# Keys with five rows innermost, three more places for expert pieces, combine transposes at the stores

## The chip, the core and the metric

The kernel runs on one core of one Trainium2 chip. The metric is the device time of one execution in microseconds (us). Three runs of the kernel before gave 885.25, 886.37 and 886.41, median 886.37. In this text PE is TensorE, PEld its weight loads, DVE is VectorE, ACT is ScalarE, POOL is GpSimd and SP is SyncE; L320 is line 320 of the kernel.

## What is computed

A linear attention over 8 batches, 8 heads, 576 positions of 64 dimensions (4608 tokens of 512), a gated feed-forward layer and a soft mixture of 8 experts, each with 4 slots:

```
q_s = softmax of q over the 64 dimensions; k_s = softmax of k over the 576 positions
kv = einsum('bhsd,bhse->bhde', k_s, v);  x = einsum('bhsd,bhde->bhse', q_s, kv)
x = x.transpose(0, 2, 1, 3).reshape(4608, 512)
x = (silu(x @ w_gate) * (x @ w_val)) @ w_out          # 512 -> 1536 -> 512
logits = x @ phi                                       # 4608 x 32 slots
d = softmax of logits over the tokens;  c = softmax over the slots
slot_input = d.T @ x                                   # 32 x 512, 4 slots an expert
slot_out[e] = max(slot_input[e] @ w1[e], 0) @ w2[e]    # w1 512 x 1024, w2 1024 x 512
out = c @ slot_out
```

The gate and value weights and w_out arrive in float64 and are made float32 on the chip.

## The kernel before

The 4608 tokens are ten blocks: eight of 512 and two of 256 (numbers 8 and 9). For each block and each of twelve tiles i of the 1536 hidden columns, a step "pair n i" runs twelve matmuls for g and twelve for v (L563: high and low halves of x against high and low halves of W, each in fp32r), Silu on ACT (L570) and a product on DVE (L572) that leaves hT. w_out is never applied to the tokens: wp = w_out @ phi gives the logits straight from hT (step lg, L626), and w_out returns only in slot_in (step si, L891), which reads it from three tiles wo_sb of two 512 KB halves each.

Before the pairs of a block come its attention steps. For each batch b and pair of heads p: the maximum of k over the batch's positions (kmax: a reduce over five rows in a partition, L320, a transpose kpT, L323, a second reduce), a matmul that copies the maximum to all partitions (kmbp, L331), a subtract on DVE (L334), exp on ACT (L338), and kv (L348): for five rows i and four 32-column groups one weight load of 32 columns and one matmul of 65 columns, the four groups side by side in the array. krs and kvbd (L354 to 356) make the block-diagonal weights from it. q is made in qa, qb and qt (L367 to 431; DVE and POOL), and px (L458, L460) gives x, split into high and low.

In the first 120 us the twelve W tiles are also built from float64 bits (steps wa, wb, wc; L486 to 508) and split into high and low (wh L521, wl L525).

After the pairs of a block, its logits go through the dispatch softmax with running maxima (pa L638, pb, pc with the dh matmuls L718, pd). At the end stand ue (transposed U), si, then for expert e: ea (h, L913), eb (transposes h1Tp), ec (y, L949), where y of all experts gathers in one PSUM bank; fin adds up the groups of y with the matrix rep (L972, L973) into st; em (L989 to 997) forms the output with st and cT and stores it in 18 DMAs of 512 KB on SP. cT is the transposed combine weight, made by ca (cs, L741, L743) and cb (cTp transposes on PE, L753, copied by L755).

The experts' w1 and w2 are 64 halves of 512 KB, loaded by DMAs on POOL's queue (L773). Where a half goes is PLACE: seven places "tl", thirteen "s8" tiles of two halves (the pool that also holds W; a tile is free when the last pair that reads the W tile has run), six halves in hN. These are the first NL = 39 halves; the other 25 are loaded by ea and ec as each expert piece is used up.

The order of everything is a table written out by hand, PROGRAM: a string of step names; each time a name occurs, that step runs on to its next yield. Nothing else orders the engines but semaphores between producers and consumers, and the tile pools' waits for a place.

Of the kernel before, what the change touches and what calls it, by code (L numbers as in the profile page):

```python
# [40 lines left out]
def rows(n):  # L41
# [13 lines left out]
    kexp 0 1, qt 0 1, qa 0 3, qb 0 2, qt 0 0, kexp 0 1, kexp 0 2, qb 0 2, qb 0 3, kv 0 1, wb 0, qt 0 1, kexp 0 3,
    kn 1 1, qt 0 2, kexp 0 2, qb 0 3, wa 0 4, kv 0 2, kv 0 1, qb 0 3, kexp 0 3, qt 0 2, qt 0 3, wa 1 5, kv 0 2, wb 0,
    w 8, kexp 0 3, wb 0, qt 0 3, kv 0 3, wa 1 5, wb 1, x 0 0, wc 0, w 9, kv 0 3, wa 2 2, x 0 1, wb 1, wb 1, x 0 0,
    x 0 2, x 0 1, x 0 0, wc 1, wh 0, x 0 1, x 0 3, x 0 2, wb 2, wa 2 2, wb 2, x 0 2, x 0 3, wb 2, wh 1, x 0 3, wc 2,
    wa 3 3, wl 0 v, wa 3 3, wb 3, pair 0 0, wa 4 4, wl 1 g, wb 3, wb 3, wh 2, wb 4, wa 4 4, pair 0 0, wb 4, wc 3,
    const rep, pair 0 0, wb 4, qa 1 0, pair 0 1, wa 5 5, wc 4, pair 0 0, qa 1 1, pair 0 0, wh 3, wb 5, wa 5 5, wb 5,  # L60
    pair 0 1, qa 1 0, wl 2 v, qa 1 1, pair 0 1, wl 3 g, wh 4, wb 5, wa 6 2, pair 0 2, qa 1 0, qa 1 1, pair 0 1,
    wa 6 2, wc 5, wl 4 v, pair 0 1, wb 6, wa 7 3, pair 0 2, wb 6, qa 1 0, pair 0 2, wb 6, wh 5, qa 1 1, kmax 1 0,
    wa 7 3, pair 0 3, wc 6, wb 7, qb 1 0, wb 7, wb 7, kmax 1 0, pair 0 3, wl 5 g, qb 1 1, kmax 1 0, pair 0 3,
    pair 0 2, qb 1 0, pair 0 2, kmax 1 1, kexp 1 0, pair 0 4, wh 6, wc 7, kexp 1 0, qb 1 1, kexp 1 0, pair 0 3,
    qb 1 0, kmax 1 1, pair 0 4, wl 6 v, qb 1 1, pair 0 3, wa 8 4, kmax 1 1, qb 1 0, wa 8 4, qb 1 1, qb 1 0, wb 8,
    kv 1 0, pair 0 4, wb 8, qb 1 1, kexp 1 1, pair 0 5, vn 1 2, wb 8, kn 1 2, kv 1 0, wh 7, wc 8, kexp 1 1, wa 9 5,
    pair 0 5, qt 1 0, pair 0 4, kexp 1 1, q 1 2, wl 7 g, wb 9, pair 0 4, wb 9, pair 0 6, wa 9 5, kmax 1 2, pair 0 5,
    w 11 1, wb 9, kmax 1 2, kv 1 1, kmax 1 2, pair 0 6, wh 8, wc 9, qa 1 2, vn 1 3, kn 1 3, kv 1 1, pair 0 6,
    pair 0 5, wl 8 v, pair 0 5, qa 1 2, wh 9, kexp 1 2, x 1 0, qa 1 2, kexp 1 2, pair 0 7, wa 10 4, qa 1 2, qt 1 1,
    kexp 1 2, wl 9 g, wb 10, q 1 3, wb 10, x 1 1, pair 0 6, qb 1 2, pair 0 7, pair 0 6, x 1 0, qb 1 2, wa 10 4, x 1 0,  # L70
    qb 1 2, kmax 1 3, x 1 1, wa 11 5, kv 1 2, wb 10, kmax 1 3, pair 0 8, vn 2 0, wa 11 5, kn 2 0, qa 1 3, wc 10,
    pair 0 7, wb 11, wb 11, pair 0 8, wb 11, pair 0 8, qa 1 3, o 0, qb 1 2, wh 10, wc 11, qa 1 3, kmax 1 3, x 1 1,
    pair 0 9, kv 1 2, pair 0 7, qa 1 3, wh 11, o 1, pair 0 8, pair 0 7, wl 10 v, qb 1 2, qb 1 3, pair 0 8, kexp 1 3,
    pair 0 9, wl 11 g, kexp 1 3, qt 1 2, pair 0 9, qb 1 3, x 1 2, kmax 2 0, qb 1 3, kexp 1 3, pair 0 10, q 2 0,
    qb 1 3, pair 0 9, qb 1 3, pair 0 9, x 1 2, qt 1 3, oa 0, kv 1 3, x 1 2, q 2 1, pair 0 10, pair 0 10, kv 1 3,
    vn 2 1, kn 2 1, ob 0, ob 0, oa 0, x 1 3, pair 0 10, oa 1, pair 0 11, qa 2 0, pair 0 10, ob 0, qa 2 0, x 1 3, oa 1,
    x 1 3, oc 0, pair 0 11, qa 2 0, qa 2 1, pair 0 11, ob 1, ob 1, qa 2 0, o 2, ob 1, pair 1 0, qa 2 1, qb 2 0,
    pair 0 11, oc 1, qa 2 1, pair 0 11, qb 2 0, pair 1 0, pair 1 0, qa 2 1, o 3, qb 2 0, qb 2 0, qb 2 1, pair 1 1,
    qb 2 0, pair 1 0, pair 1 0, qt 2 0, qb 2 1, q 2 2, pair 1 1, qb 2 1, pair 1 1, qb 2 1, qb 2 1, pair 1 2, pair 1 1,
# [140 lines left out]
    em 1, em 3, em 2, em 1, em 3, em 3, em 3, em 2, em 2, em 2, em 2, em 3, em 3, em 2, em 4, em 3, em 3, em 2, em 4,  # L220
    em 4, em 3, em 5, em 4, em 3, em 5, em 5, em 5, em 4, em 4, em 4, em 4, em 5, em 5, em 4, em 6, em 5, em 5, em 4,
    em 6, em 6, em 5, em 7, em 6, em 5, em 7, em 7, em 7, em 6, em 6, em 6, em 6, em 7, em 7, em 6, em 8, em 7, em 7,
    em 6, em 8, em 8, em 7, em 8, em 7, em 8, em 8, em 8, em 8, em 8, em 8
"""


# [861 lines left out]
```

## Time and profile before

| | us |
|---|---|
| median of three runs | 886.37 |
| the profiled execution | 884.27 |
| its span | 882.5 |
| PE busy | 820.1 (93%) |
| PE weight loads busy | 617.8 (70%) |
| DVE busy | 528.0 (60%) |
| ACT busy | 402.3 (46%) |
| POOL busy | 275.9 (31%) |

The profile is of one execution. The busy time of an engine is read beside the stretch in which it lies: the program has a start (attention of the first block, W's conversion), a long middle (the pairs), and a tail (slot_in, experts, stores), which the windows separate. The chain of waits goes back from the last instruction to what released each step. PE's matmuls are pipelined, so busy PE does not mean PE at its peak. Time of the profile is counted from the start of the span; the profiled execution is 1.8 us longer than it.

### The profile page before, as it was taken

How to read it: one execution, taken by the hardware profiler on the slowest of the kernel's cores; microseconds unless marked ns; L12 is line 12 of the kernel's file. 1: busy time of each engine (PE TensorE's matmuls, PEld its weight loads, DVE VectorE, ACT ScalarE, POOL GpSimd, SP SyncE). 2: the span in 40 equal slices, each digit the busy share in tenths (PEclk: the TensorE clock that was granted, in tenths of full speed). 3: DMA queues.
4: the chain of work that ended last, by engine and by line, in shares of the span. 5: the costliest groups of instructions: out<-in, count | busy, mean ns of one | idle time of the engine just before them, and what ended most of it. 6: DMA issues, size and time to landing. Idle time of an engine off the chain costs nothing.

```text
span 882.5 us, 14883 instructions
## 1 busy us (share of the span) xinstructions
PE 820.1 (93%) x5664; PEld 617.8 (70%) x5664; DVE 528.0 (60%) x1060; ACT 402.3 (46%) x532; POOL 275.9 (31%) x413
## 2 busy tenths in 40 slices
...
GB/s 346 412 50 79 180 199 130 97 116 196 94 121 145 167 145 138 162 176 112 112 129 177 115 88 168 159 151 80 102 106 82 111 114 151 387 332 287 411 168 354
DMA packets 104215, 151.04 MB, mean 171 GB/s; under 512 B 60240, under 2 KB 73936, under 8 KB 101072
## 3 DMA queue, kind: packets, MB, share of 16 engines
...
HBM read 105.22 MB, written 25.17 MB: 148 GB/s over the span
## 4 chain that ended last, share of the span: by engine, by line
PE 81%; DVE 11%; DMA 3%; issue 2%; ACT 1%; POOL 1%; SPq 0%; POOLq 0%; ACTq 0%; DVEq 0%
PE g L563 31%; PE v L563 31%; PE lg L626 3%; PE dh L718 3%; DVE ost L493 2%; PE kv L348 2%; DMA piece<-in_w_dram 2%; PE px L458 2%; DVE ost L500 2%; PE px L460 1%; DVE ost L496 1%; PE h L913 1%; PE o L989 1%; DVE W L525 1%; PE y L949 1%
## 5 line engine op out<-in xcount | busy, mean ns | idle before, releaser
L563 PE MATMUL g<-x,W 128*128 128x512 f32 (+1 forms) x1440 | 329.3, 378 | 6.7 <-DVE W L525 6.7
L563 PE MATMUL v<-x,W 128*128 128x512 f32 (+1 forms) x1440 | 326.3, 376 | 0.0
L563 PEld LDWEIGHTS g<-x,W 128*128 128x128 f32 x1440 | 250.4, 190 | 72.4 <-issue 15.5
L563 PEld LDWEIGHTS v<-x,W 128*128 128x128 f32 x1440 | 251.3, 190 | 54.7 <-issue 9.1
L572 DVE TENSOR_TENSOR hT<-hT,v 128x512 f32<-128x512 f32 (+1 forms) x120 | 75.4, 629 | 180.1 <-PE v L563 161.1
L570 ACT ACTIVATE hT<-g 128x512 f32<-128x512 f32 (+1 forms) x120 | 66.4, 555 | 190.5 <-PE g L563 189.9
L373 POOL TENSOR_TENSOR qd<-qd,qsd 128x512 f32<-128x512 f32 (+1 forms) x72 | 71.9, 1003 | 73.4 <-DVE qsd L396 40.8
L570 ACT ACT_TABLE_LOAD x62 | 79.5, 1283 | 10.5 <-PE g L563 9.5
L367 POOL COPY qsd<-qsd 64x16 f32<-64x16 f32 (+1 forms) x144 | 37.9, 263 | 99.6 <-DVE qsd L392 48.0
L303 POOL DMA_DIRECT2D vn<-in_vn_dram x24 | 13.5, 562 | 153.6 <-PE kv L348 151.4
L583 DVE STREAM_TRANSPOSE hB<-hT 128x512 f32<-128x512 f32 (+1 forms) x78 | 53.4, 686 | 4.3 <-PE wpT L534 2.3
L773 POOL DMA_DIRECT2D piece<-in_w_dram x58 | 30.5, 530 | 58.3 <-PE hNp L609 19.4
L464 ACT ACTIVATE x<-px 128x512 fp32r<-128x512 f32 (+1 forms) x40 | 22.0, 552 | 48.8 <-PE px L460 33.7
L320 DVE TENSOR_REDUCE kpart<-kn 128x128 f32<-128x640 f32 x32 | 40.9, 1277 | 4.5 <-DMA kn<-in_kn_dram 4.5
L338 ACT ACTIVATE kn<-kn 128x640 f32<-128x640 f32 x32 | 23.6, 738 | 36.9 <-DVE kn L334 36.2
L309 POOL DMA_DIRECT2D qd<-in_qd_dram x24 | 13.7, 572 | 71.2 <-DVE qsT L427 55.2
L334 DVE TENSOR_TENSOR kn<-kn,kmbp 128x640 f32<-128x640 f32 x32 | 25.9, 808 | 16.4 <-PE kmbp L331 16.4
L402 ACT ACT_TABLE_LOAD x24 | 30.8, 1283 | 8.9 <-DVE qst L384 8.5
L338 ACT ACT_TABLE_LOAD x22 | 28.2, 1283 | 14.5 <-DVE kn L334 13.2
L427 DVE STREAM_TRANSPOSE qsT<-qd 128x512 f32<-128x512 f32 (+1 forms) x36 | 23.2, 646 | 18.3 <-PE px L460 7.2
L508 POOL TENSOR_TENSOR ost<-ost,f 128x1024 int32<-128x1024 int32 x10 | 25.8, 2583 | 19.7 <-DVE ost L500 5.3
L348 PEld LDWEIGHTS kv<-vn,kn 128*32 128x32 f32 x1280 | 20.6, 113 | 13.3 <-issue 7.5
(150 smaller groups left out, 941.6 us busy)
## 6 DMA issues: line engine op xcount, KB each, us to landing
...
```

The source lines that it names most:

```text
L320: nc.vector.tensor_reduce(out=part, in_=kn_t[b, p].rearrange("p i d -> p d i"), axis=AX, op=ALU.max)
L338: nc.scalar.activation(out=t, in_=t, func=ACTF.Exp)
L348: nc.tensor.matmul(acc[r:r + 32, :], lhsT=ek[:, i, 64 * j + 32 * h:64 * j + 32 * h + 32], rhs=vv[:, i, j, :], start=(i == 0), stop=(i == S ...
L367: nc.gpsimd.tensor_copy(out=st[64 * g:64 * g + 64, o + 1], in_=st[64 - 64 * g:128 - 64 * g, o])
L373: nc.gpsimd.tensor_tensor(out=a, in0=a, in1=s, op=op)
L402: nc.scalar.activation(out=a, in_=a, func=ACTF.Exp)
L563: nc.tensor.matmul(gv[j], lhsT=W[i][:, w, k, j, :], rhs=x[:, k, :], start=(k == 0 and w == 0 and x is xh), stop=(k == KT - 1 and w == 1),)
L570: nc.scalar.activation(out=s, in_=g, func=ACTF.Silu)
L572: nc.vector.tensor_tensor(out=s, in0=s, in1=v, op=ALU.mult)
L583: nc.vector.transpose(out=hB[n, i // w][:, :, i % w, :], in_=s.rearrange("p (b j) -> p b j", j=32))
L626: nc.tensor.matmul(lg[n][32 * g:32 * g + 32, :], lhsT=wp[:, i, :], rhs=hs[:, g] if n < NSP else hs[g], start=(r == 0), stop=(r == 2), tile ...
L773: nc.gpsimd.dma_start(out=ap, in_=(w1 if r < 4 else w2)[e, r % 4])
```

## The change

Five things change. (1) The keys' tile is [128, 128, 5] in place of [128, 5, 128]: the host lays the five rows that a partition holds next to one another, so the reduce reads them contiguously, the subtract broadcasts the maximum along the innermost axis, and kv's weights are 32 columns 5 elements apart. (2) The three Wo tiles are places for six more halves, after slot_in, so NL is 45 and 19 halves are left to ea and ec. (3) The combine steps ca and cb move from among the experts to their end. (4) finish copies each half of y once in float32 (one half on ACT, one on DVE) and sums it with one float32 matmul, in place of a high and a low fp32r part and two; the last block's logits are treated likewise. (5) The whole PROGRAM table is written anew: pairs of a block run in other orders of i, which go with when each W tile is freed, pieces are asked for in another order, and the attention steps stand elsewhere among the pairs.

```
-            t = at.tile([128, ST, 128], F32, tag="kn", name="kn")
-        else:
-            t = start_tile("kn0", [128, 2 * ST, 128])[:, ST * (p - 2):ST * (p - 1)]
+            t = at.tile([128, 128, ST], F32, tag="kn", name="kn")
+        else:
+            t = start_tile("kn0", [128, 2, 128, ST])[:, p - 2]
...
-        nc.vector.tensor_reduce(out=part, in_=kn_t[b, p].rearrange("p i d -> p d i"), axis=AX, op=ALU.max)
+        nc.vector.tensor_reduce(out=part, in_=kn_t[b, p], axis=AX, op=ALU.max)
...
-            out=t, in0=t, in1=mb.unsqueeze(1).to_broadcast([128, ST, 128]), op=ALU.subtract
+            out=t, in0=t, in1=mb.unsqueeze(2).to_broadcast([128, 128, ST]), op=ALU.subtract
...
-                        acc[r:r + 32, :], lhsT=ek[:, i, 64 * j + 32 * h:64 * j + 32 * h + 32], rhs=vv[:, i, j, :],
+                        acc[r:r + 32, :], lhsT=ek[:, 64 * j + 32 * h:64 * j + 32 * h + 32, i], rhs=vv[:, i, j, :],
...
+        if n == NB - 1:
+            l32 = lsp[n] = hp.tile([128, nt], F32, tag="h", name="l32")
+            nc.scalar.activation(out=l32, in_=acc, func=ACTF.Copy)
+            return
...
+        if n == NB - 1:
+            nc.tensor.matmul(l, lhsT=rep.bitcast(F32), rhs=lsp.pop(n), start=True, stop=True)
+        else:
...
-    PLACE = ["tl"] * TL + ["s8"] * TS + ["hN"] * 6
-    NL = len(PLACE) + TS
+    PLACE = ["tl"] * TL + ["s8"] * TS + ["hN"] * 6 + ["s8"] * 3
+    NL = len(PLACE) + TS + 3
...
-        j = i + min(max(i - TL, 0), TS)
+        j = i + PLACE[:i].count("s8")
...
-            nc.scalar.activation(out=yh[:, c], in_=y[:, c], func=ACTF.Copy)
-            yield
-            nc.vector.tensor_tensor(out=yl[:, c], in0=y[:, c], in1=yh[:, c].bitcast(F32), op=ALU.subtract)
-            yield
-            nc.tensor.matmul(so[:, c], lhsT=rep, rhs=yh[:, c], start=True, stop=False)
-            nc.tensor.matmul(so[:, c], lhsT=rep, rhs=yl[:, c], start=False, stop=True)
+            if k:
+                nc.vector.tensor_copy(out=yf[:, c], in_=y[:, c])
+            else:
+                nc.scalar.activation(out=yf[:, c], in_=y[:, c], func=ACTF.Copy)
+            yield
+            nc.tensor.matmul(so[:, c], lhsT=rep.bitcast(F32), rhs=yf[:, c], start=True, stop=True)
...
-    kn = seq_tiles(kn, 128)
+    kn = seq_tiles(kn, 128).swapaxes(3, 4)
```

What the new table does to the queues is shown at three places. The first is PE's queue in the kernel before where block 3 passes to block 4 (x_2229 is block 3's x, x_3122 block 4's; a row is a run of equal instructions):

```order
L563 MATMUL v<-x_2229,W 128x512
L348 MATMUL kv<-vn,kn 32x65 x20
L626 MATMUL lg<-hT,wp 32x512 x4
L458 MATMUL px<-qsT,kvbd_93 128x256
L460 MATMUL px<-qsT,kvbd_92 128x256
L626 MATMUL lg_2736<-h0T,wp 32x512 x4
L563 MATMUL g<-x_3122,W 128x512
```

The same place after the change (x_2175 is block 3's x, x_3015 block 4's; the lines left out are the other matmuls of the pair's g and v):

```order
L563 MATMUL v<-x_2175,W 128x512
L458 MATMUL px<-qsT,kvbd_93 128x256
L460 MATMUL px<-qsT,kvbd_92 128x256
L323 MATMUL kpT<-ident,kpart 128x128
L563 MATMUL g<-x_2175,W 128x512
...
L563 MATMUL v<-x_2175,W 128x512
...
L323 MATMUL kpT<-ident,kpart 128x128
L331 MATMUL kmbp<-ident,kmax 128x128
L563 MATMUL g<-x_3015,W 128x512
```

Before, the last px of block 4 stands directly ahead of block 4's first g, with four logits matmuls between; now a whole pair of block 3 stands between.

The second place is POOL's queue from the end of the attention steps on, before; the DMAs of Wo's tiles are wo_sb, those of the experts' halves are piece and hN:

```order
L373 TENSOR_TENSOR qd<-qd,qsd 128x256
L773 DMA piece<-in_w_dram 128x1024 x6
L829 DMA wo_sb<-wo_91 128x2x1024
L773 DMA piece<-in_w_dram 128x1024 x11
L773 DMA hN_6639<-in_w_dram 128x1024 x3
L773 DMA piece<-in_w_dram 128x1024 x16
L773 DMA hN_6639<-in_w_dram 128x1024 x3
L773 DMA piece<-in_w_dram 128x1024 x25
```

The same after:

```order
L836 DMA wo_sb<-wo_91 128x2x1024 x2
L780 DMA piece<-in_w_dram 128x1024 x2
L836 DMA wo_sb<-wo_91 128x2x1024
L780 DMA piece<-in_w_dram 128x1024 x15
L780 DMA hN_6749<-in_w_dram 128x1024 x3
L780 DMA piece<-in_w_dram 128x1024 x16
L780 DMA hN_6749<-in_w_dram 128x1024 x3
L780 DMA piece<-in_w_dram 128x1024 x25
```

Both queues issue 64 halves and the three loads of Wo. After the change, two loads of Wo stand ahead of the first halves, and the last row, of 25 halves, holds the six that go to Wo's places, ahead of the 19 that ea and ec load.

The third place is PE's queue from slot_in to the first output, before:

```order
L891 MATMUL si<-wo_sb,uT 32x128 x32
L753 MATMUL cTp<-ident,cs 128x128 x4
L900 MATMUL siTp<-ident,si_sb 128x128
L753 MATMUL cTp<-ident,cs 128x128 x4
L913 MATMUL h_7529<-piece,siT 32x256 x4
L913 MATMUL h_7536<-piece,siT 32x256 x4
...
L753 MATMUL cTp<-ident,cs 128x128 x4
L931 MATMUL h1Tp<-ident,h_sb 128x128 x2
...
L949 MATMUL y<-piece,h1T 32x512 x8
L972 MATMUL so<-yh,rep 128x256
L973 MATMUL so<-yl,rep 128x256
...
L989 MATMUL o<-st,cT 128x512 x36
```

And after:

```order
L898 MATMUL si<-wo_sb,uT 32x128 x32
L907 MATMUL siTp<-ident,si_sb 128x128
L920 MATMUL h_7508<-piece,siT 32x256 x4
L920 MATMUL h_7513<-piece,siT 32x256 x4
...
L956 MATMUL y<-piece,h1T 32x512 x8
L760 MATMUL cTp<-ident,cs 128x128 x8
L956 MATMUL y<-piece,h1T 32x512 x8
L760 MATMUL cTp<-ident,cs 128x128 x8
L979 MATMUL so<-yf,rep 128x256
L760 MATMUL cTp<-ident,cs 128x128 x8
...
L760 MATMUL cTp<-ident,cs 128x128 x2
L995 MATMUL o<-st,cT 128x512 x34
```

Before, eight of the 36 transposes stand between slot_in and the end of the first experts' first matmuls, and the rest among the experts. After, they stand behind the last h, and around the two sums of fin.

## Rows read from the trace of the kernel before

**Rows 1.** the page's totals (busy us, share, instructions) and the chain by engine
```profile
PE 820.1 (93%) x5664; PEld 617.8 (70%) x5664; DVE 528.0 (60%) x1060; ACT 402.3 (46%) x532; POOL 275.9 (31%) x413
...
PE 81%; DVE 11%; DMA 3%; issue 2%; ACT 1%; POOL 1%; SPq 0%; POOLq 0%; ACTq 0%; DVEq 0%
```

**Rows 2.** busy us of each engine by stretch, granted clock, DMA share, GB/s
```profile
20.00:40.00 20.00, 10.29 (x145) 8.16 (x138) 19.62 (x29) 14.43 (x19) 11.54 (x8) 0.85 1.02 410
...
100.00:120.00 20.00, 18.19 (x135) 14.03 (x137) 18.51 (x28) 14.00 (x16) 15.03 (x15) 1.00 0.60 190
120.00:240.00 120.00, 120.00 (x748) 94.25 (x737) 81.28 (x133) 65.86 (x73) 52.81 (x66) 1.00 0.39 132
...
360.00:380.00 20.00, 15.42 (x142) 9.91 (x141) 14.88 (x31) 7.85 (x11) 7.54 (x15) 0.91 0.66 195
```

**Rows 3.** the chain of waits from 0 to 137 us, by line
```profile
by line: DVE ost L493 13.5%; DVE ost L500 10.7%; issue 8.6%; DVE ost L496 7.4%; PE g L563 7.3%; PE v L563 6.1%; DVE W L525 5.9%; DVE kpart L320 4.3%; DMA q<-in_q_dram 3.8%; DVE kn L334 3.7%; DVE hT L572 2.4%; POOL ost L508 2.3%; DVE x L466 
```

**Rows 4.** the chain of waits in the tail (start us, us, what)
```profile
790.48 1.45 PE v L563 x12
...
819.76 9.67 DMA piece<-in_w_dram
...
829.97 7.25 DMA piece<-in_w_dram
...
847.35 1.97 PE y L949 x16
...
853.45 4.09 PE o L989 x9
```

**Rows 5.** groups by shape: busy us, mean ns of one, idle before and releaser
```profile
L563 PEld LDWEIGHTS v<-x,W 128*128 128x128 f32 x1440 | 251.3, 190 | 54.7 <-issue 9.1
...
L570 ACT ACT_TABLE_LOAD x62 | 79.5, 1283 | 10.5 <-PE g L563 9.5
...
L320 DVE TENSOR_REDUCE kpart<-kn 128x128 f32<-128x640 f32 x32 | 40.9, 1277 | 4.5 <-DMA kn<-in_kn_dram 4.5
...
L348 PE MATMUL kv<-vn,kn 128*32 128x65 f32 x1280 | 25.9, 228 | 2.8 <-ACT kn L338 2.8
L334 DVE TENSOR_TENSOR kn<-kn,kmbp 128x640 f32<-128x640 f32 x32 | 25.9, 808 | 16.4 <-PE kmbp L331 16.4
...
L348 PEld LDWEIGHTS kv<-vn,kn 128*32 128x32 f32 x1280 | 20.6, 113 | 13.3 <-issue 7.5 <-ACT kn L338 4.1 <-ACT ost L486 0.4
...
L392 DVE TENSOR_REDUCE qsd<-qd 128x16 f32<-128x512 f32 x28 | 18.8, 670 | 0.8 <-DMA qd<-in_qd_dram 0.8
...
L989 PEld LDWEIGHTS o<-st,cT 128*128 128x128 f32 x36 | 9.9, 317 | 6.0 <-DVE ob L992 2.6 <-ACT ob L994 1.7 <-DVE st L977 1.1
```

**Rows 6.** what PE waited for, 120 to 780 us (total, times, longest)
```profile
PE px L458 <- DVE qsd L396: 4.3, 1, 4.3
```

**Rows 7.** the chain of waits where block 3 passes to 4
```profile
361.77 2.95 PE g L563 x12
...
365.80 2.75 PE v L563 x12
...
378.12 3.29 PE g L563 x12
...
381.88 2.72 PE v L563 x12
```

**Rows 8.** busy time by stretch in the tail
```profile
800.00:805.00 5.00, 4.09 (x51) 2.45 (x51) 2.15 (x10) 0.83 (x3) 1.24 (x3) 0.50 0.83 296
805.00:810.00 5.00, 5.00 (x102) 3.67 (x94) 1.41 (x4) 1.69 (x4) 0.92 (x2) 0.95 0.20 80
810.00:815.00 5.00, 5.00 (x66) 2.77 (x66) 1.33 (x5) 2.88 (x7) 3.78 (x8) 1.00 0.91 312
...
825.00:840.00 15.00, 13.52 (x150) 5.41 (x148) 0.69 (x6) 2.47 (x6) 5.17 (x10) 1.00 1.03 409
```

**Rows 9.** what POOL's queue waited for, 715 to 845 us
```profile
POOL piece L773 <- PE h L913: 10.1, 5, 7.4
```

More of the change, by code (lines that the diff above doesn't have):

```diff
@@ L55 @@
[L55 to L79, printed above, removed]
@@ L220 @@
[L220 to L223, printed above, removed]
+    const ident, kn 0 0, kn 0 1, kn 0 2, kn 0 3, q 0 0, q 0 2, vn 0 0, const mask, q 0 1, vn 0 1, q 0 3, kmax 0 0,
@@ new lines @@
+    kexp 2 0, pair 1 3, pair 1 3, q 2 1, kexp 2 0, kexp 2 0, kv 2 1, pair 1 3, pair 1 5, kv 2 1, kn 2 2, pair 1 3,
+    vn 2 2, qa 2 1, qa 2 1, op 0, qa 2 1, pair 1 5, pair 1 5, op 0, qa 2 1, kmax 2 2, qb 2 1, op 0, pair 1 5,
+    kmax 2 2, pair 1 2, kmax 2 2, pair 1 5, oa 2, op 0, qb 2 1, qb 2 1, oa 2, ob 2, kexp 2 2, kv 2 0, qb 2 1,
+    kexp 2 2, qb 2 1, pair 1 9, kv 2 0, kexp 2 2, kn 2 3, ob 2, vn 2 3, ob 2, x 2 0, oc 2, kv 2 2, x 2 0, qt 2 1,
+    pair 1 2, pair 1 2, kv 2 2, x 2 0, kn 3 1, o 4, kmax 2 3, vn 3 1, q 2 2, op 1, pair 1 2, kmax 2 3, pair 1 6, oa 3,
@@ new lines @@
+    qt 2 3, pair 1 10, oa 5, op 3, x 2 2, q 3 1, oa 5, kmax 3 0, qa 3 0, x 2 3, ob 5, op 3, ob 5, kmax 3 0, x 2 3,
+    pair 1 10, op 3, qa 3 0, pair 1 10, kmax 3 0, x 2 3, qa 3 0, kmax 3 1, qa 3 0, ob 5, pair 2 4, u 0, qb 3 0,
+    pair 1 10, oc 5, pair 1 10, qb 3 0, pair 2 4, pair 2 4, qb 3 0, qb 3 0, qb 3 0, kexp 3 0, kmax 3 1, op 4,
+    pair 2 4, ua 0, pair 2 0, qa 3 1, qt 3 0, ua 0, qa 3 1, kexp 3 0, q 3 2, qa 3 1, kexp 3 0, ub 0, pair 2 0, ub 0,
+    ub 0, qa 3 1, pair 2 0, kmax 3 1, uc 0, pair 2 3, op 4, qb 3 1, pair 2 0, pair 2 0, ud 0, op 4, u 1, qb 3 1,
```

319 lines of the change are left out of this document (168 added, 151 removed).

## The prediction

> **What bounds the kernel now.** I read the page's totals and chain first, then the engines' busy time stretch by stretch, then the shapes of the instructions that the edits touch, then the chain of waits at the two places where TensorE (PE) is not full, and last what DMA moves in the tail. The totals say PE: 820 of 882.5 us, and 81% of the chain that ended last [rows 1]. But a share of the span is an average over three stages with different limits.
>
> In the first stage, to about 120 us, DVE is busy 19.6 of 20 us and PE 10.3; just before 120 us it is still 18.5 against 18.2 [rows 2]. The chain there runs through DVE: the three lines that build W's float32 from its bits (L493, L500, L496) 31.6%, the W low parts 5.9%, kpart 4.3% [rows 3]. In the second stage, the pairs from 120 to 780 us, PE is busy 120 of 120 us in a stretch; the window 360 to 380 is the exception, with 15.42 of 20 and a granted clock of 0.91 [rows 2]. In this stage a microsecond in which PE does nothing is a microsecond of the end. The third stage starts when the last v ends at 790.48 + 1.45 = 791.93, here called E. Then the experts wait for pieces of their weights, twice visibly in the chain: 9.67 and 7.25 us [rows 4]; then come the sum over groups and the stores.
>
> **The change part by part.**
>
> *Keys innermost, the reduce.* Each of 32 kpart reduces reads 640 elements with a stride and takes 1277 ns; a contiguous reduce of 512 takes 670 [rows 5]. Scaled by elements that is 838 ns less the fixed part, so I take 0.80 us: 0.48 saved, 15 us of DVE in all. Only the start is bound by DVE. Eight of the 32 stand ahead of the last low part of W on DVE: 8 x 0.48 = 3.8 us. Summing every DVE instruction that stands ahead of that last low part, each at its duration in the trace of before, gives 90.9 us in the old order and 86.6 in the new, 4.3 less, so the new order adds 0.5 to the 3.8. In the end of the stage PE follows this sum, so I take **-4.3**. Bounds: 0, if the waits for W's conversion on POOL set the pace, and -10, if the pairs which stand earlier in the new order let PE fill more of its holes.
>
> *The subtract and the exp.* The subtract now broadcasts along the innermost axis. Before shows 808 ns for the same 640 elements [rows 5]; no row shows this broadcast. If it were as slow as the strided reduce, 0.47 us more for each, the eight in the start would lose the 3.8 us again; a gain has no source, since every element of the larger operand is still read. I take 0 and keep +3.8. Exp is an element by element pass over the whole tile and stays.
>
> *Keys innermost, the weights of kv.* The 1280 kv loads take 32 columns that are now 20 bytes apart. Before has no such load of 32 columns. The nearest row is the emit load of 128 columns 16 bytes apart: 317 ns against 190 for contiguous ones of pairs [rows 5], 127 ns for 128 columns or 32 ns for 32. The loads of kv are busy 20.6 us together and their matmuls 25.9 [rows 5], since the four column groups of a step are loaded side by side. If the four stay side by side, 320 steps x 32 ns = 10.2 us make 30.8 us of loads, 4.9 us over the matmuls that cover them. If they do not, it is 1280 x 32 ns = 41 us. Below, 0: neither a stride nor an order makes a load shorter. The side-by-side reading is nearer to the row, which has 20.6 us for 1280 loads of 113 ns, so I take **+2**, between 0 and 4.9, and keep 41 for a rival.
>
> Two rules of the Trainium skill part here. Its page SBUF — State Buffer, in the note on SBUF "cachelines", says that a line has 16 bytes and that each access which goes to a new line pays; that speaks for the reduce (512 bytes apart before, 4 now) and against kv's weights (4 bytes apart before, 20 now). By it the kv term would be at the 4.9 end and the sum 2.9 us higher. Its page TensorE: Matmul & The Clock Gate, section LDWEIGHTS, has the time of a load hang on its columns alone; by it the term would be 0 and the sum 2 us lower. The emit loads, 317 against 190 ns with equal columns [rows 5], agree with the first and not with the second.
>
> *The order of pairs.* Within a block the pairs now run shuffled, and what stands between two blocks is another set. Before, the four px of block 4 end directly ahead of its first g; PE waits 4.3 us for DVE's qsd ahead of the last px [rows 6], and the first g starts at 378.12 although the last v of the block before ended at 365.80 + 2.75 = 368.55 [rows 7]. In the window PE is idle 4.58 us, and a clock of 0.91 over 20 us costs 1.8 more [rows 2]: 6.4. In the new order a whole pair, its g and its v, and the kpT and kmbp of another batch stand between the last px and that g, so that the DVE chain has some 6 us of cover: **-6.4**, bounds -6.4 and 0. The other boundaries: adding the trace's durations over PE's order from a block's last px to its first g, the old order has 1.7 (this one) to 13.5 us of PE work, the new one 1.2 (block 0 to 1) to 19.5. That 1.2 is the one lead shorter than the old worst; if it stalls like block 3 to 4 it costs 6.4; DVE is just past its busy stage there. I take **+1.5**, a quarter of it, and keep +6.4.
>
> *Fewer switches on PE.* After a run of 32-column matmuls (kv, lg, dh) the next chain takes 2.95 us for what otherwise takes 2.72 [rows 7]. I count 97 such runs in PE's old order and 84 in the new: 13 x 0.23 = **-3.0**, bounds 0 and -4.4 (0.34 with what the run itself loses).
>
> *Wo's places and the pieces.* 45 halves of 512 KB, not 39, are queued ahead of the experts, and 19, not 25, on their release. At 409 GB/s a half takes 1.28 us. In the tail DMA falls from 409 to 296, 80 and 312 GB/s between 800 and 815 [rows 8], where the remaining halves wait in POOL's queue for h to give places back, once for 7.4 us [rows 9]: 1.4 + 4.0 + 1.2 = 6.6 us of full rate lost. Six more halves are 7.7 us and fill it, provided that slot_in releases Wo in time; each pair of them now waits for the third of slot_in that reads it, and behind them on POOL nothing else is queued than later pieces. So the last half lands 6.6 us sooner. In the chain, y then follows that landing [rows 4].
>
> *Combine transposes at the stores.* 36 transposes leave the path of the first h; they stood beside the waits of 9.67 and 7.25, which hid them, so their going gains nothing beyond what the DMA allows. At the end some twelve of them stand between the last y and the first o, with their copies; finish itself loses a subtract and a matmul for each half. Finish took from 847.35 + 1.97 = 849.32 to 853.45, 4.1 us [rows 4]; with the transposes I take 5.0, +0.9. The last block's logits in float32 save a subtract of DVE, 0.3. Together the tail: -6.6 + 0.9 - 0.3 = **-6.0**; bounds -10 (no loss left anywhere) and +1 (the landing does not move, and finish lengthens). From the first o the 18 stores are unchanged, 29 us to the end.
>
> ACT gets four more activation table loads of 1.28 us each by its order; ACT is busy 46% of the span [rows 1], and its idle time hides them. Were each on the path, they would cost 5.
>
> **Sum.** -4.3 + 2.0 - 6.4 + 1.5 - 3.0 - 6.0 = -16.2 us. The profiled execution took 884.27 us (a span of 882.5 and 1.8 around it), so it would be 868.1; the median of the runs shown is 2.1 above that execution, so the median to be expected is 886.37 - 16.2 = 870.2, rounded to **870**.
>
> **The rivals.**
>
> *The strided weights do not load side by side.* They are slower than before from the point where they cost 16.2 + 2.0 + 1.8 = 20 us, 15.6 ns a load. At 32 ns a load it is 41 us in place of the 2: 870 + 39 = 909; at half of that, 889. For it: the row of the strided load, and kv's matmuls, too short to cover a longer load. Against it: the loads of four groups overlap today.
>
> *The gain is given back inside the pairs.* The new order stalls at block 0 to 1 (+4.9 over my term), the stall of block 3 to 4 moves instead of going (+6.4): 881. For it: the leads were counted, not the DVE time they need; against it: DVE is busy only 81 of 120 us there [rows 2].
>
> *DMA does not move in the tail.* The extra halves wait longer for Wo than I think, the landing stays: 870 + 6.6 = 877.
>
> *The reduce is not faster, or the subtract loses it.* Then the start does not move: 870 + 4 = 874.
>
> **How the numbers follow.** The forecast with its own range, 858 to 877, gets 0.57, the third and fourth rival being inside it at its upper end; better than 858 gets 0.07; the second rival, 877 to 884.6, gets 0.15; a change within 0.2% (884.6 to 888.1, about what a measurement can tell from none) gets 0.05; the strided weights get 0.13, and other mishaps above 888 get 0.03. So faster 0.79, same 0.05, slower 0.16. The range 855 to 885 leaves out a little below and the slower cases.
>
> **What would show it.** The reduce near 0.8 us; kv's 1280 loads longer than 113 ns while a kv group of 40 stays near 0.6 us; no PE hole at block 3 to 4 and none at 0 to 1; dense PE from about 115 us instead of 120; DMA near 409 GB/s through slot_in; y done some 51 us behind the last v instead of 57. A kv group of over 1 us, or holes of 4 us at other block ends, would make the forecast wrong.

## The result and the profile after

The kernel after took 866.11 us (median of 4 runs, 864.46 to 867.45) beside 886.01 for the kernel before on the same chip: a ratio of 0.9776, 95% interval 0.9757 to 0.9794, 19.9 us less. Run again with the last experiments it had 866.26 beside 885.37, ratio 0.9778 (0.9764 to 0.9793). The forecast was 870, range 855 to 885.

The profiled execution of after took 867.45 us, the slowest of its four runs; its span is 865.7 against 882.5, so between the two profiles there are 16.8 us to explain, not 19.9. The remaining 3.1 lie between executions: the profile of before is 1.7 below the median of 886.01 (2.1 below the 886.37 that the forecast started from), that of after 1.3 above its own.

The totals of after, which answer to [rows 1] (busy us, share, instructions; then the chain by engine):

```profile
PE 816.6 (94%) x5664; PEld 624.3 (72%) x5664; DVE 499.4 (58%) x1058; ACT 406.8 (47%) x535; POOL 271.7 (31%) x413
...
PE 84%; DVE 7%; issue 2%; ACT 2%; DMA 1%; POOL 1%; SPq 0%; POOLq 0%; DVEq 0%
```

DVE has 28.6 us less work and DMA's share of the chain fell from 3 to 1%. Where the 16.8 us went is read by stage. Busy time of each engine by stretch, granted clock, DMA share and GB/s, first of before, over longer stretches than in [rows 2]:

```profile
0.00:120.00 120.00, 87.64 (x636) 68.02 (x640) 111.50 (x149) 76.92 (x87) 77.26 (x65) 0.93 0.58 214
120.00:360.00 240.00, 240.00 (x1548) 186.07 (x1537) 149.52 (x269) 112.97 (x130) 77.38 (x108) 1.00 0.47 136
```

and of after, with the window of [rows 2]:

```profile
0.00:120.00 120.00, 94.07 (x677) 73.61 (x678) 105.39 (x152) 79.23 (x89) 75.15 (x66) 0.93 0.59 219
120.00:360.00 240.00, 238.72 (x1582) 186.12 (x1581) 139.76 (x275) 113.01 (x131) 81.02 (x119) 1.00 0.46 137
360.00:380.00 20.00, 20.00 (x135) 15.00 (x134) 15.12 (x33) 10.75 (x14) 7.33 (x15) 1.00 0.58 147
```

By 120 us PE has done 94.07 us of work instead of 87.64, at the same mean clock of 0.93: 6.4 x 0.93 = 6.0 us earlier. This lies early in the stage. From 40 to 60 us, before:

```profile
40.00:60.00 20.00, 18.92 (x74) 15.06 (x73) 19.86 (x19) 13.22 (x14) 15.09 (x9) 0.89 0.35 143
```

and after, with two windows of [rows 2]:

```profile
20.00:40.00 20.00, 15.51 (x173) 12.62 (x174) 18.82 (x29) 16.58 (x20) 9.89 (x7) 0.71 1.02 412
40.00:60.00 20.00, 20.00 (x87) 16.41 (x86) 18.33 (x22) 13.28 (x15) 12.82 (x10) 0.95 0.25 97
...
100.00:120.00 20.00, 17.98 (x112) 13.44 (x111) 16.08 (x26) 14.62 (x18) 16.28 (x15) 1.00 0.68 239
```

From 20 to 60 us, busy time times clock, it is 30.0 instead of 25.6 us; from 100 to 120 PE is no denser than before (17.98 against 18.19). From 120 to 360 us PE is full in both, but for 1.3 us of after. In the window of the old hole it goes from 15.42 us at 0.91 to 20.00 at 1.00: the 6.4 us that the prediction worked out from that row. That makes 12.4. The last v ends at 777.74 + 1.44 = 779.18, so the pairs end 12.75 us earlier; what is left to fewer runs of 32-column matmuls, slower kv loads and new stalls together is -0.35. From there to the end of the span are 86.5 us instead of 90.6: -4.1.

The shapes that the edit touched, in after (busy us, mean ns of one, idle before and its releaser; they answer to [rows 5], line numbers from L633 on are 6 or 7 higher):

```profile
L348 PE MATMUL kv<-vn,kn 128*32 128x65 f32 x1280 | 28.4, 237 | 5.3 <-DMA vn<-in_vn_dram 3.3 <-ACT kn L338 2.0
...
L334 DVE TENSOR_TENSOR kn<-kn,kmbp 128x640 f32<-128x640 f32 x32 | 25.8, 809 | 7.6 <-PE kmbp L331 7.5
L320 DVE TENSOR_REDUCE kpart<-kn 128x128 f32<-128x640 f32 x32 | 25.7, 803 | 8.0 <-DMA kn<-in_kn_dram 7.9
L348 PEld LDWEIGHTS kv<-vn,kn 128*32 128x32 f32 x1280 | 24.8, 149 | 16.8 <-issue 12.0 <-ACT kn L338 4.2 <-ACT W L521 0.4
```

The reduce takes 803 ns, as forecast (0.80 us); the subtract, 809, did not mind the other broadcast (808 before). A load of kv's weights takes 149 ns instead of 113, 36 more where the prediction had 32, but all 1280 together are busy 24.8 us, 4.2 more, where one after another they would be 190.7, and the matmuls 28.4, 2.5 more: the four column groups do load side by side. The Trainium skill's note on SBUF "cachelines" (SBUF — State Buffer) fits the faster reduce and the slower load; that a load's time hangs on its columns alone (TensorE: Matmul & The Clock Gate, LDWEIGHTS) does not.

The chain of waits where block 3 passes to block 4 (start us, us, what), after:

```profile
360.19 0.43 PE px L458 x2
360.62 0.43 PE px L460 x2
...
361.16 2.75 PE g L563 x12
363.91 2.72 PE v L563 x12
...
366.74 0.22 PE kmbp L331 x2
366.96 2.76 PE g L563 x12
```

Behind the last px stand the g and v of one more pair of block 3, 5.47 us, and the first g of block 4 starts 0.33 us behind that v. In [rows 7] 9.57 us lay between them.

The tail of after by stretch, which answers to [rows 8]:

```profile
790.00:795.00 5.00, 4.34 (x86) 3.11 (x74) 0.49 (x2) 0.28 (x1) 2.57 (x5) 0.70 1.01 397
...
805.00:810.00 5.00, 5.00 (x66) 2.24 (x58) 0.41 (x4) 1.17 (x4) 2.12 (x4) 1.00 1.03 412
...
825.00:830.00 5.00, 5.00 (x52) 2.33 (x45) 0.95 (x3) 1.59 (x4) 0.00 (x0) 1.00 0.27 105
```

DMA keeps 397 to 412 GB/s through slot_in and the experts; before it fell to 296, 80 and 312. The last packet of the experts' halves ends at 827.98 in the trace, 48.8 us behind the last v; before it ended at 845.50, 53.6 behind. The chain of the end in after, for [rows 4]:

```profile
777.74 1.44 PE v L563 x12
...
830.48 1.85 PE y L956 x16
...
832.96 1.08 ACT cT L762 x2
...
834.79 0.80 ACT cs L748 x3
835.60 0.49 ACT cT L762
...
836.99 0.86 PE o L995 x2
```

No DMA wait stands in it any more. y ends at 832.33, 53.15 us behind the last v (57.4 before), and from there to the first o are 4.7 us (4.1 before), of which ACT's copies of cT and cs take over 2.

### The profile page after: what moved, and what is told of

The parts are those of the page before. It is cut to its first block, busy times and chain, and to the rows that moved or that the text cites. A ratio compares the mean times of both kernels' runs of the same rounds, so it can differ in the third digit from the quotient of the medians.

```text
span 865.7 us, 14870 instructions
## 1 busy us (share of the span) xinstructions
PE 816.6 (94%) x5664; PEld 624.3 (72%) x5664; DVE 499.4 (58%) x1058; ACT 406.8 (47%) x535; POOL 271.7 (31%) x413
## 3 DMA queue, kind: packets, MB, share of 16 engines
q0 software_dynamic: 16176, 59.90, 19.9%
## 4 chain that ended last, share of the span: by engine, by line
PE 84%; DVE 7%; issue 2%; ACT 2%; DMA 1%; POOL 1%; SPq 0%; POOLq 0%; DVEq 0%
PE g L563 32%; PE v L563 32%; PE lg L626 3%; PE dh L725 3%; PE kv L348 2%; PE px L458 2%; PE y L956 2%; PE h L920 2%; PE px L460 1%; DVE ost L496 1%; PE o L995 1%; DVE ost L500 1%; DVE ost L493 1%; DMA f<-in_wgv_dram 1%; PE kmbp L331 1%
## 5 line engine op out<-in xcount | busy, mean ns | idle before, releaser
L563 PE MATMUL v<-x,W 128*128 128x512 f32 (+1 forms) x1440 | 321.1, 372 | 0.0
L373 POOL TENSOR_TENSOR qd<-qd,qsd 128x512 f32<-128x512 f32 (+1 forms) x72 | 69.9, 972 | 41.0 <-DVE qsd L396 17.7
L367 POOL COPY qsd<-qsd 64x16 f32<-64x16 f32 (+1 forms) x144 | 35.4, 246 | 145.1 <-DVE qsd L392 72.8
L295 POOL DMA_DIRECT2D kn<-in_kn_dram x24 | 14.0, 584 | 123.8 <-PE kv L348 63.7
L583 DVE STREAM_TRANSPOSE hB<-hT 128x512 f32<-128x512 f32 (+1 forms) x78 | 50.6, 673 | 1.5 <-DMA hN<-hB 0.3
L348 PEld LDWEIGHTS kv<-vn,kn 128*32 128x32 f32 x1280 | 24.8, 149 | 16.8 <-issue 12.0
L348 PE MATMUL kv<-vn,kn 128*32 128x65 f32 x1280 | 28.4, 237 | 5.3 <-DMA vn<-in_vn_dram 3.3
L320 DVE TENSOR_REDUCE kpart<-kn 128x128 f32<-128x640 f32 x32 | 25.7, 803 | 8.0 <-DMA kn<-in_kn_dram 7.9
L414 DVE TENSOR_REDUCE qsd<-qd 128x16 f32<-128x512 f32 (+1 forms) x36 | 22.2, 615 | 13.7 <-ACT qd L402 13.5
```

What stands on the lines that cost most here:

```text
L348: nc.tensor.matmul(acc[r:r + 32, :], lhsT=ek[:, 64 * j + 32 * h:64 * j + 32 * h + 32, i], rhs=vv[:, i, j, :], start=(i == 0), stop=(i == S ...
L367: nc.gpsimd.tensor_copy(out=st[64 * g:64 * g + 64, o + 1], in_=st[64 - 64 * g:128 - 64 * g, o])
L373: nc.gpsimd.tensor_tensor(out=a, in0=a, in1=s, op=op)
L563: nc.tensor.matmul(gv[j], lhsT=W[i][:, w, k, j, :], rhs=x[:, k, :], start=(k == 0 and w == 0 and x is xh), stop=(k == KT - 1 and w == 1),)
L583: nc.vector.transpose(out=hB[n, i // w][:, :, i % w, :], in_=s.rearrange("p (b j) -> p b j", j=32))
```

## The experiments

All medians here are beside the kernel before on the same chip, at 885.4 to 885.8 us; medians of one kernel, taken on two occasions, differ by up to 0.7. So small effects are also read from the profiles, as the end of the k-th pair of the program (120 in all) less that of after. The kernel after, profiled again (e12), gives -2.6 to +0.6 in the first seven pairs, then -1.0 to -0.8 until pair 78 and -0.1 to the end: an offset from the start, and one step of 0.8 at pair 79. Other runs whose start is that of after have larger offsets: at pair 13, e10 is at +0.4 and e8 at -2.3. A slope that goes on, or a step well over 0.8, is therefore read; an offset is not. Tails differ too, by 1 to 2 us, with the granted clock in slot_in (e5).

**e1, the old layout of the keys in the new order.**

```
-            t = at.tile([128, 128, ST], F32, tag="kn", name="kn")
+            t = at.tile([128, ST, 128], F32, tag="kn", name="kn")
...
-        nc.vector.tensor_reduce(out=part, in_=kn_t[b, p], axis=AX, op=ALU.max)
+        nc.vector.tensor_reduce(out=part, in_=kn_t[b, p].rearrange("p i d -> p d i"), axis=AX, op=ALU.max)
...
-                        acc[r:r + 32, :], lhsT=ek[:, 64 * j + 32 * h:64 * j + 32 * h + 32, i], rhs=vv[:, i, j, :],
+                        acc[r:r + 32, :], lhsT=ek[:, i, 64 * j + 32 * h:64 * j + 32 * h + 32], rhs=vv[:, i, j, :],
```

Expected: 

> The kernel after with the keys' old layout alone put back (five rows outermost; strided reduce, contiguous weights for kv); the order stays. Theory: the reduce pays only in the start, the weights cost all along. The 8 reduces of the start get 0.47 us each longer (1277 against 803 ns), 3.8 us later; the 32 groups of 40 kv matmuls get 0.075 us shorter, 2.4 us earlier: together +1.4 us, 867.5. Rival A, the start is not set by DVE: -2.4, 863.7. Rival B, kv's longer loads are hidden: +3.8, 869.9.

Measured: 866.92 us, ratio 0.9779 (0.9764 to 0.9795); the pairs end 0.8 us later in the profile. The size is the theory's, near nothing. The layout has no part in the 19.9 us that could be told from noise, either way.

**e2, contiguous weights and a fast reduce.**

```
-        nc.vector.tensor_reduce(out=part, in_=kn_t[b, p].rearrange("p i d -> p d i"), axis=AX, op=ALU.max)
+        nc.vector.tensor_reduce(out=part, in_=kn_t[b, p].rearrange("p i d -> p (i d)").rearrange("p (d i) -> p d i", i=ST), axis=AX, op=ALU.max)
```

(on e1). Expected: 

> The kernel after with the keys' old layout (contiguous weights for kv, the subtract broadcasting as before), but the reduce reads the tile's elements five by five as they lie, so it takes the maximum over other elements than the softmax wants; its time is that of the contiguous reduce. So the strided weights alone are taken away. Theory: 32 groups x 0.075 us = -2.4 us, 863.7, with kv's loads back from 149 to 113 ns. Rival: the loads lie beside other work, 0 us, 866.1.

Measured: 865.79 us, ratio 0.977 (0.9756 to 0.9784). The loads are back at 113 ns:

```profile
L320 DVE TENSOR_REDUCE kpart<-kn 128x128 f32<-128x640 f32 x32 | 25.7, 803 | 7.3 <-DMA kn<-in_kn_dram 7.3
L348 PE MATMUL kv<-vn,kn 128*32 128x65 f32 x1280 | 25.6, 227 | 4.9 <-DMA vn<-in_vn_dram 2.8 <-ACT kn L338 2.0
...
L348 PEld LDWEIGHTS kv<-vn,kn 128*32 128x32 f32 x1280 | 21.1, 113 | 16.5 <-issue 10.5 <-ACT kn L338 4.3 <-ACT wo_st L486 0.4
```

The ends of the pairs move ahead of those of after in a steady slope, -0.2 us at pair 13, -0.6 at 29, -1.2 at 57, -1.8 at 89, -1.7 at the last: 1.5 us over the 24 groups of kv of batches 2 to 7, 0.06 each. The median moves by 0.3 to 0.5, too little to tell by itself. So the strided loads do cost, 1.5 us by the slope and 2.8 by the matmuls' busy time (28.4 against 25.6). Against e1, which differs in the reduce alone, it is 0.7 us at pair 13, within the offsets, and 2.5 at the last: in the start of this order the slow reduce shows no 3.8. The other 1.8 are steps of 0.3 at pair 18, 0.8 at 50, 0.1 at 54 and 0.7 at 79. They are not shown to be the reduce's: e11 has the slow reduce from batch 2 on and stays within 0.1 us of e2 from pair 13 to the last, and the step at 79 is in e12 as well, whose reduces are all fast.

**e3, 39 places.**

```
-    PLACE = ["tl"] * TL + ["s8"] * TS + ["hN"] * 6 + ["s8"] * 3
-    NL = len(PLACE) + TS + 3
+    PLACE = ["tl"] * TL + ["s8"] * TS + ["hN"] * 6
+    NL = len(PLACE) + TS
...
-    si, piece 17, ue, piece 17, si, piece 18, piece 18, si, piece 19, si, piece 19, si, ea 1
+    si, ue, si, si, si, si, ea 1
```

(pieces 28, 27 and 26 take the names 17, 18 and 19, and the experts' steps six more turns for the loads that they issue.) Expected: 

> The kernel after without Wo's three places: 39 halves ahead of the experts and 25 on release, the combine transposes at the end as in the kernel after. Theory: DMA sets the tail, and six halves of 1.28 us start only when the experts release places; the last half lands 5 to 7 us later and y with it: +5.5 us, 871.6, with a hole in DMA ahead of the experts as in the kernel before. Rival: PE's own work for h and y sets the tail since PE has no visible wait there: +0.5 us, 866.6.

Measured: 872.61 us, ratio 0.9856 (0.9838 to 0.9875), 6.4 above after. Busy time by stretch in its tail, the pairs ending at 779.5:

```profile
789.00:794.00 5.00, 4.63 (x92) 3.57 (x94) 0.74 (x5) 0.83 (x3) 1.20 (x3) 0.62 1.01 380
794.00:799.00 5.00, 4.09 (x81) 2.64 (x73) 0.64 (x2) 0.08 (x1) 2.41 (x5) 1.00 0.34 116
...
814.00:829.00 15.00, 9.82 (x82) 3.23 (x76) 0.28 (x2) 0.77 (x2) 4.02 (x8) 0.77 1.02 408
829.00:834.00 5.00, 5.00 (x60) 1.85 (x53) 0.57 (x4) 0.00 (x0) 0.00 (x0) 1.00 0.33 131
```

and its chain there:

```profile
802.14 11.09 DMA piece<-in_w_dram
...
813.77 9.99 DMA piece<-in_w_dram
```

The hole in DMA is back, 116 GB/s from 794 to 799, and both waits are back in the chain. From 814 to 829 PE is busy 9.82 of 15 us and its granted clock falls to 0.77. The theory stands: with the rest of the new tail as it is, the six places are worth 6.4 us, more than the whole tail gained (4.1 between the profiles).

**e4, the whole old tail** behind the new pairs: e3, and the old program from the step ue on (the old order of experts, ca and cb among them; finish keeps its new form).

```
...
-    ec 7, cb 4, fin, cb 3, cb 4, fin, cb 3, cb 5, fin, cb 5, fin, fin, ca 7, cb 6, ca 9, ca 7, fin
...
+    ea 0, cb 1, ca 4, ea 1, ea 0, ea 0, ea 1, ea 1, cb 2, ea 0, ea 0, ea 1, cb 2, ea 1, ea 0, ca 5
```

Expected: 

> The kernel after with the whole old tail behind its own pairs: 39 halves, the old order of experts, the combine transposes among the experts. Theory: the difference of the two tails in the profiles, 4.0 us, comes back: +4.0, 870.1; against the run with 39 places alone it is 1.5 better, because the transposes stand beside DMA waits and no longer at the end. Rival: the transposes cost PE as much among the experts as at the end, so that it is the same as with 39 places alone.

Measured: 869.41 us, ratio 0.981 (0.9791 to 0.9829): 3.3 above after, 3.2 better than e3. The theory's direction holds, with more than its 1.5 between the two. Of the 3.2 the order of the experts may have a part, since both moved at once; that is not separated. The new tail as a whole is worth 3.3 us by this, about half of what its places are worth alone.

**e5, the new layout alone in the old order.** The edit of the change's parts (1) on the kernel before, the reverse of e1's diff. Expected: 

> The kernel before with the new layout of the keys alone, the old order. Theory: -3.8 us from eight reduces of the start and +2.4 us from kv's weights: -1.4, 884.6. Rival: in the old order the start has other waits (POOL, W's conversion), so that the reduce gives nothing: +2.4, 888.4.

Measured: 883.74 us beside 885.5, ratio 0.9981 (0.997 to 0.9992): 1.7 us, at the theory's 1.4. In the profile (less before, pair by pair) the pairs are 1.7 us earlier at pair 9 and then lose it in a slope, -1.0 at 33, -0.5 at 73, -0.2 at the last: by the end of the pairs nothing of the layout is left. The profile's span is 1.9 us shorter all the same, and that lies in the tail, in which no keys are handled: 88.8 us from the last v to the end instead of 90.6. The stretch of slot_in, for [rows 8]:

```profile
800.00:805.00 5.00, 4.08 (x104) 3.02 (x101) 2.15 (x10) 0.83 (x3) 1.09 (x3) 0.99 0.89 297
```

The granted clock is 0.99 there, where the profile of before has 0.50. e6, with the old layout and the same tail, is like e5 in both: 0.97 in the stretch as far behind its last v, and 88.8 us. So these 1.8 us are not the layout's, and why the median keeps 1.7 us is open. Starts of the new order alone differ by more than the 1.7 at pair 9 (2.7 us between e8 and e10); before and e6, with the old order and layout, agree to 0.1. So that the reduce gives the 1.7 is plausible and not shown.

**e6, the last product of block 3 behind the steps of q** (kernel before; DVE's order):

```
-L572 hT, L583 hB, L414 qsd, krs, kvbd, L320 kpart, L418 qsd, L419, L640 llo, L392, L427 qsT
+L414 qsd, krs, kvbd, L418 qsd, L419, L392, L427 qsT, L396, L572 hT, ..., L583 hB, L320 kpart, L640 llo
```

Expected: 

> The kernel before, where block 3 passes to block 4: on DVE the last product of block 3, its transpose, the next batch's kpart and the low part of the logits stand behind the steps of q for the last px of block 4, and on PE the logits of block 3 stand behind that px. Theory: the chain of q (exp, sum, swap, reciprocal, multiply, transpose) is what the wait consists of, and the four DVE instructions lengthen it by 2 us: the last px starts at about 372.8 us instead of 374.8: -2 us, 884.0. Rival: the chain's own length sets it, 0 us, 886.0.

Measured: 885.24 us, ratio 1.0004 (0.9993 to 1.0015): nothing. The chain of waits says why:

```profile
369.97 0.51 POOL vn L303
...
370.52 0.54 POOL kn L295
...
374.05 1.21 PE px L458 x2
...
376.11 3.32 PE lg L626 x16
```

The last px starts at 374.05, 0.7 us sooner and not 2: POOL issues the loads of vn and kn, 1.05 us, ahead of the swap of q's sums (L367), so DVE is not what the chain waits for. And the logits that now stand behind px run at the lower clock behind the hole, 3.32 us for 16, where before eight of them ran within the hole. In the profile the pairs from the 49th on even end 1.9 us later than before; the span hides it, because the tail is 1.7 shorter, as in e5. The rival's number came; its reason, the chain's own length, has POOL's two issues in it.

**e7, more runs of 32-column matmuls.**

```
                 start=(r == 0), stop=(r == 2), tile_position=(0, 32 * g),
             )
+            if n >= NSP and g == 1: yield
```

(and the second half's turn behind the next g or v in the program). Expected: 

> The kernel after with the four logits matmuls of a group of 24 steps cut in two with one chain of twelve pair matmuls in between (23 of 24 fall so): the work is the same, PE has 23 more runs of 32-column matmuls. Theory: each run costs the next chain 0.23 us and loses 0.1 in itself: 23 x 0.23 to 0.34 = +5.3 to +7.8 us, 871.4 to 873.9. Rival: the longer reading of the chain behind such a run is how the profile models ends: 0 us, 866.1.

Measured: 896.04 us, ratio 1.0109 (1.0091 to 1.0127): 30 us slower than after, where 5 to 8 were expected. The chain of waits around one group, in after and then here:

```profile
258.49 2.72 PE g L563 x12
261.20 1.00 PE lg L626 x8
262.20 2.96 PE v L563 x12
```

```profile
257.83 2.72 PE g L563 x12
260.55 0.98 PE lg L626 x4
261.53 2.95 PE v L563 x12
264.48 0.98 PE lg L626 x4
```

Two column groups of logits (x4: a float32 matmul is two records) take 0.98 us, as long as the four (x8) of after, 1.00. Four groups run for the price of one, so a split run takes its time twice: 18 x 0.98 for the blocks of 512, 5 x 0.56 for those of 256 (the duration there), 20.4 us, and 23 x 0.2 for the changes of tile (2.95 instead of 2.72 for the chain behind) make 25.0. The profile's pairs end 25.5 us later than those of after, or 27.4 if the 1.9 by which they are ahead until the first split, an offset, are added. The sum leaves 5 of the 30 us unexplained. That is no test of the 0.23 that the prediction took; it shows that the price of splitting is the lost company of the other groups.

**e8, the layout by batch.** New for batches 0 and 1, old for 2 to 7.

```
...
+        if b < 2:
+            m = mb.unsqueeze(2).to_broadcast([128, 128, ST])
+        else:
+            t = t.rearrange("p d i -> p i d")
+            m = mb.unsqueeze(1).to_broadcast([128, ST, 128])
```

Expected: 

> The kernel after with the new layout of the keys for batches 0 and 1, whose attention lies in the start, and the old layout for batches 2 to 7. Theory: the start keeps its fast reduces, DVE has room for the strided ones later, and kv's weights are contiguous in 24 of 32 groups: 24 x 0.075 = -1.8 us, 864.3. Rival: the 24 slower reduces, 0.47 us each, make a chain late at a block's end: 0 to +4 us, 866 to 870.

Measured: 865.18 us, ratio 0.9775 (0.9755 to 0.9795); not told apart from after. The profile of e11, which has the same pairs, moves ahead of after by 1.6 us from pair 13 to the last, the slope of e2 and near the theory's 1.8; the profile here moves 1.2 by pair 78 and then has the step of e12.

**e9, the cover at block 3 to 4 removed.** In the program the v of pair 3 11 and the g and v of pair 3 9 stand ahead of x 4 3 (the px and x steps of block 4):

```
-    x 4 3, pair 3 8, pair 3 11, ..., x 4 3, qt 4 1, x 4 3, q 5 0, x 4 1, ..., pair 3 9, x 4 1, ..., pair 3 9
+    pair 3 11, pair 3 9, pair 3 9, x 4 3, pair 3 8, ..., x 4 3, qt 4 1, x 4 3, q 5 0, x 4 1, ..., x 4 1
```

Expected: 

> The kernel after, where block 3 passes to block 4: the v of pair 3 11 and the g and v of pair 3 9 stand ahead of the two last px pairs of block 4 on PE, not between and behind them; the other engines' orders are the same. Theory: the work between the px and the first g of block 4 is what took the old hole away; without it PE waits for the transpose of q that follows the first px pair (0.7 us), for the high and low part of x behind the second (1.3 us), and runs at the lower clock behind the hole: +2 to +4 us, 868 to 870, all of it between pairs 48 and 50. Rival: the hole went because q's chain runs earlier, and the cover does not matter: 0, 866.1.

Measured: 869.1 us, ratio 0.9822 (0.9804 to 0.984), 2.8 above the kernel after measured beside it. In the profile the pairs up to 46 are at -0.2 and from pair 49 on at +3.3: the whole of it is here. The chain of waits:

```profile
364.55 0.43 PE px L458 x2
...
370.31 2.73 PE g L563 x12
```

and PE's instructions that waited there, and what DVE did (start us, us, engine, idle before in brackets):

```profile
366.21 0.70 PE L458 MATMUL px<-qsT,kvbd 128*128 128x256 f32 x2 [0.80 <-DVE qsT L427]
...
368.57 0.33 PE L323 MATMUL kpT<-ident,kpart 128*128 128x128 f32 x1 [1.11 <-DVE kpart L320]
369.85 0.46 PE L331 MATMUL kmbp<-ident,kmax 128*128 128x128 f32 x2 [0.95 <-DVE qsd L396]
```

```profile
367.49 0.29 DVE L326 TENSOR_REDUCE kmax<-kpT 128x1 f32<-128x128 f32 x1
...
369.02 0.68 DVE L466 TENSOR_TENSOR x<-px,x 128x512 fp32r<-128x512 f32 x1
369.63 0.17 DVE L396 TENSOR_TENSOR qsd<-qsd 128x16 f32<-128x16 f32 x1
```

PE has no chain of pair matmuls between 364.55 and 370.31, 5.76 us, of which it is idle 2.9. The first wait is for the transpose of q, 0.80 us, as expected (0.7). The last is the one expected for the low part of x behind the second px, though the view names qsd: PE's weight queue had its wait behind it at 369.74, before qsd ended (369.80) and just after the low part of x did (369.70); kmbp needs one of the three PSUM places that px and kpT use, and the last px holds it until then. Its maximum (L326) was ready long before. The 1.11 us for kpart had not been expected. The lower clock had been, and did not come: the granted clock is 1.00 from 365 to 375 us. So the pair of cover hides 3.5 us; the other 2.9 of the old 6.4 are other differences of the order ahead of it, not separated.

**e10, the sum over groups first.**

```
-        for k, c in enumerate((slice(0, DM // 2), slice(DM // 2, DM))):
...
+        nc.scalar.activation(out=yf[:, cs[0]], in_=y[:, cs[0]], func=ACTF.Copy)
+        nc.vector.tensor_copy(out=yf[:, cs[1]], in_=y[:, cs[1]])
+        yield
+        for c in cs:
+            nc.tensor.matmul(so[:, c], lhsT=rep.bitcast(F32), rhs=yf[:, c], start=True, stop=True)
...
-    ec 7, cb 4, fin, cb 3, cb 4, fin, cb 3, cb 5, fin, cb 5, fin, fin, ca 7, cb 6, ca 9, ca 7, fin
+    ec 7, fin, fin, fin, fin, fin, em 0, ..., cb 3, cb 3, em 2, ..., cb 4, cb 4, em 3
```

Expected: 

> The kernel after, with finish written as both copies of y, both sums, then the rest, directly behind the last y, and the combine steps for blocks 3 to 9 (seven of ten) among the stores' own steps, each ahead of the block that needs it. Theory: from the last y to the first o there are 5.3 us, of which copies of cT and cs on ACT are over 2 us; the stores are set by DMA and hide the combine steps: the first store and the end come 2.5 us earlier, 863.6. Rival: the stores wait for cT, or ACT sets their pace: 0 or slower, 866 to 868.

Measured: 864.98 us, ratio 0.9772 (0.9757 to 0.9786); the kernel after measured beside it 866.26. From the last y (832.1 starts) to the first o (836.2) it is 4.1 us where after has 5.3: 1.2 of the 2.5 expected, because the two sums stand together (1.17 us) and the four steps of st behind them still follow one another (1.7). The intervals overlap.

**e11, both.** e10 and e8 in one. Expected: 

> The last run's tail together with the keys' new layout for batches 0 and 1 only. Theory: the two add, -2.5 and -1.8 us: 861.8. Rival: what is won ahead of the experts does not move the end because DMA has its own start: -2.5 alone, 863.6.

Measured: 865.07 us, ratio 0.9773 (0.9758 to 0.9788). The two do not add in the median; no version here is shown to beat the kernel after.

**e12, the kernel after again.** Expected: 

> The kernel after, unchanged, beside the three others: 866.1 us, to within 1 us. It says how far the medians of two calls and two profiles of one kernel differ; every theory expects no change.

Measured: 866.26 us, ratio 0.9778 (0.9764 to 0.9793), as told above.

## Why the prediction was right, and where a step of it failed

The forecast of 870 had the direction, and its sum of -16.2 us stands beside 16.8 between the two profiles. The median lay 3.9 lower, of which 3.1 are the executions that happened to be profiled. That the sum comes within 0.6 us is luck in part: the start gave 1.7 more than its term and the tail 1.9 less. Step by step:

*The start, -4.3, measured -6.0.* The size is near; the step "In the end of the stage PE follows this sum" failed. The sum is that of DVE's work ahead of the last low part of W. Its totals of 90.9 and 86.6 are not what the traces have: DVE is busy 105.1 us ahead of that low part before and 98.8 after. The low part starts at 109.57 us instead of 112.21, only 2.6 earlier, and PE gains from 20 to 60 us and not at the end of the stage; its last wait in the start is at 124.67 us, so the sign "dense PE from about 115 us" did not come either. The 3.8 us of eight reduces show as 1.7 us by pair 9 in the old order (e5) and 0.7 by pair 13 in the new (e2 against e1), neither clear of the offsets between executions. So the new order gives most of it, which the text had only as the reason of its bound of -10; which of the moves does it was not tried. The other runs with this start stand between +0.4 and -2.3 us to after at pair 13, so the -6.0 of this one profile could be -5.6 to -8.3.

*kv's weights, +2.0, measured +1.5 (e2's slope) to +2.8 (busy time).* Right, with its mechanism: 36 ns longer loads, side by side. The rival of 41 us, which had 0.13, did not come.

*Block 3 to 4, -6.4, measured -6.4.* Right in size, and the hole went as forecast. But the named cover holds only 3.5 of it (e9); the other 2.9 belong to moves that the text did not name. In the old order the wait of q ran through POOL's queue as much as DVE's (e6), which the text did not see.

*New stalls, +1.5, measured +1.3*: one wait of kmbp for kmax between 120 and 240 us is all that PE lacks there.

```profile
125.96 0.49 PE L331 MATMUL kmbp<-ident,kmax 128*128 128x128 f32 x2 [1.28 <-DVE kmax L326]
```

The 12th pair ends at 123.59 us and the 13th begins at 126.20, so the wait lies at block 0 to 1, where the text had it. That the size fits is luck: it was a quarter of a stall of 6.4.

*Fewer runs, -3.0.* Not shown by itself. With kv and the stalls the sum was to be +0.5; the difference of the profiles leaves -0.35 for the three. Taking off +1.5 to +2.8 and +1.3, the runs come out at -3 to -4.5, by difference alone, with whatever else moved. The experiment meant for it measured another thing (e7).

*The tail, -6.0, measured -4.1* between the two profiles, in both of which the granted clock falls in slot_in (0.50 from 800 to 805 us before, 0.70 from 790 to 795 after); 3.3 by the medians of e4. The mechanism is right: DMA no longer starves, and taking the places away costs 6.4 us (e3). The term "the last half lands 6.6 us sooner" is the step that was mis-sized: 53.6 - 48.8 = 4.8. The text held the first piece's start fixed, and counted only the hole from 800 to 815, where DMA before also fell to 150 GB/s from 785 to 790. From the issue of the first piece to the last packet it is 9.8 us less (91.4 instead of 101.2), but that piece was issued 47.6 us ahead of the last v before (744.4 against 792.0) and 42.6 ahead after (736.6 against 779.2); in after POOL waits 10.3 us ahead of it for a v of the pairs. Finish was sized at +0.9 and measured 4.66 - 4.13 = +0.5.

*The subtract and ACT's table loads at nothing:* right: the subtract takes 809 ns against 808; ACT is busy 406.8 us, 4.5 more, and no wait for it grew into the chain of the pairs.
